# Ordering GpSimd's tensor operations behind VectorE's in a planned attention and mixture-of-experts kernel

## The chip, the cores and the metric

One core of a Trainium2 chip runs the whole program. The metric is device time in microseconds; three runs of the kernel before took 801.38, 801.94 and 803.85 us, so the median is 801.94 us. The profile is of one further execution, 803.63 us long.

## The reference: what is computed

Attention over 4 batches of 8 heads, 576 positions and 64 channels, in which heads 0 to 3 look at the last 32 positions and heads 4 to 7 at every 32nd; its output, 2304 rows of 512, goes through four experts, each weighted per row:

```python
scores = np.where(mask, scale * q @ k.T, -1e9)
attn = softmax(scores); x = (attn @ v)            # -> 2304 x 512
p = domain_probs / (domain_probs.sum(-1, keepdims=True) + 1e-09)
for e in range(4):                                # w1[e] 512 x 1024, w2[e] 1024 x 512
    out += p[:, e:e + 1] * (np.maximum(x @ w1[e], 0.0) @ w2[e])
```

## The kernel before

Everything is float32. A product of two float32 operands is made of three matmuls on rounded halves: each operand is split into a high half (ScalarE rounds it, `AF.Copy`) and a low half (the operand minus its high half), and high x high, high x low and low x high are added in PSUM. The low half is a subtraction of two SBUF operands, and either VectorE or GpSimd may do it; the same holds for most sums and differences of operands.

The rows are treated in three parts. The first 384 rows go through the experts by plain products while attention runs (to about 199 us). The other 1920 are two parts of 896 and 1024 rows (199 to about 492 us, and to the end). Those use a scheme of seven products for a 2 x 2 block product, on halves of the rows (448 or 512 columns of a matmul): per unit (half an expert, 8 units a part) seven products for the hidden layer and seven for the output, each for two halves of the output columns, six matmuls each. [...]

In part 1 the sums of the weights are made too (lines 855, 859 and 862), spilled to DRAM by SP (lines 912 and 921) and read back in part 2 (1149, 1364). GpSimd's queue also issues the DMAs that add a group's output to DRAM (1332, 1335).

The order of all this is not written by hand: the class `Plan` is a list scheduler in Python that runs when the program is built. Each operation has an engine (or a choice: kind `VP` may go to VectorE or GpSimd, kind `AD` to ScalarE or VectorE), an estimated duration, a priority and its dependences. `walk` steps through simulated time: for each engine it looks for the operations that could start first, lets `elsewhere` refuse those which the other engine would finish earlier, picks one by priority, and books it. At the end all operations are issued in order of planned time, each into its engine's queue. The engines then run their queues in order, with semaphores for true dependences only, so that the real overlap of two engines is not bound to the planned one.

Operations with two SBUF inputs carry `two`. Where GpSimd and VectorE both run such an operation, the plan lengthens them (`took`, `slowed`). `harm` estimates how much time VectorE would have in such operations during a GpSimd one; from 45 us on (`EARLY`) `elsewhere` refuses GpSimd an operation by it:

```python
if e == "POOL" and s >= self.EARLY and harm(o, s) > self.SHARE * o.dur[0]:
    return True
```

with `SHARE` 0.0. VectorE's pick goes by priority, except that operations on PSUM go first while GpSimd is known to be busy for more than `NEAR` with an operation on two SBUF inputs.

Of the kernel before, what the change touches and what calls it, by code (L numbers as in the profile page):

```python
# [17 lines left out]
MIX = 2.42  # L18
# [19 lines left out]


class Op:  # L40
    __slots__ = ("eng", "dur", "fn", "nxt", "wait", "ready", "prio", "bank", "start", "end", "moe", "cols", "idx", "xfer", "two", "pre", "kind", "lead", "early", "lag")


class Plan:
# [6 lines left out]
    BUSY, WARM = 3200, 2000  # L51
    LANES, RING = 8, 2048
    DEEP = 1.26
    SHARE = 0.0
    EARLY = 45.0
    NEAR = 0.3
    DEEPER = 5.0
    ROW = 1.0
    SWITCH = 0.17
# [2 lines left out]
    ENGINES = ("PE", "ACT", "DVE", "POOL", "SP")  # L62
    FLEX = {"VP": ("DVE", "POOL"), "AD": ("ACT", "DVE")}

    def __init__(self, banks, mix):
        self.ops = []
        self.number = 0
        self.writer = {}
        self.readers = {}
        self.banks = banks  # L70
        self.mix = mix
        self.swing = self.SWING
# [43 lines left out]
    def run(self, idle):  # L116
# [7 lines left out]
        for n, fn in self.walk():  # L124
            if n:
                idle(n, fn)
            else:
                fn()

    def walk(self):  # L130
        avail = {e: [] for e in self.ENGINES}
        moe = [o for o in self.ops if o.moe]
# [9 lines left out]
        began = False  # L142
        out = []
        seen = {}

        def warm(t):
            k = int(t / self.TICK)
            return k > 0 and seen.get(k - 1, 0) >= self.WARM
# [40 lines left out]
        def when(o):  # L189
            t = o.ready  # L190
            if o.xfer is not None and o.start is None:
                t = max(t, wire - (self.DEEP if wire < 200 else self.DEEPER))
            for i, key in enumerate(o.bank):
                n = len(allocs[key[0]]) - self.banks[key[0]] + i
                if n >= 0:
                    for p in self.readers.get(allocs[key[0]][n], ()):
                        if p.start is None:
                            return None
                        t = max(t, p.end + self.SYNC)
            return t  # L200
# [9 lines left out]
        def took(o, e, s):  # L210

            d = o.dur
            if o.eng in self.FLEX:
                d = d[self.FLEX[o.eng].index(e)]
            if o.two and e in ("DVE", "POOL"):
                other = "POOL" if e == "DVE" else "DVE"
                x = free[other] - s
                if x > 0 and last[other] is not None and last[other].two:
                    d = slowed(s, x, d) if e == "DVE" else d + min(x, d) * 0.2
            return d  # L220

        def harm(o, s):

            t, end = max(free["DVE"], s), s + o.dur[1]
            both = 0.0
            if last["DVE"] is not None and last["DVE"].two:
                both = max(0.0, t - max(s, last["DVE"].start))
            for y in sorted((y for y in avail["DVE"] if y is not o and y.ready < end and y.eng != "AD"), key=lambda y: (y.prio, y.idx)):
                if t >= end:
                    break  # L230
                t = max(t, y.ready)
                d = y.dur[0] if y.eng == "VP" else y.dur
                if y.two:
                    both += max(0.0, min(end, t + d) - t)
                t += d
            return 0.65 * both

        def elsewhere(o, e, s):

            if o.eng not in self.FLEX:  # L240
                return False
            a, b = self.FLEX[o.eng]
            x = b if e == a else a
            if e == "POOL" and s >= self.EARLY and harm(o, s) > self.SHARE * o.dur[0]:
                return True
            est = free[x]
            for y in avail[x]:
                if y is not o and (y.prio, y.idx) < (o.prio, o.idx) and y.eng not in self.FLEX and y.ready < s + 1.0:
                    est += y.dur
            est = max(est, o.ready)  # L250
            return est + took(o, x, est) < s + took(o, e, s) - 1e-9

        def transfer(s, dur, parts):
# [23 lines left out]
        while left:  # L277
            best = None
            for e in self.ENGINES:
                f = free[e]  # L280
                cand = [(max(t, f), o) for t, o in ((when(o), o) for o in avail[e]) if t is not None]
                cand = [c for c in cand if not elsewhere(c[1], e, c[0])]
                if e == "PE" and moe and not moe[-1].wait:
                    t = when(moe[-1])
                    if t is not None:
                        cand.append((max(t, f), moe[-1]))
                if not cand:
                    continue
                s0 = min(c[0] for c in cand) + 1e-9
                if e == "DVE" and s0 > self.EARLY and last["POOL"] is not None and last["POOL"].two and free["POOL"] > s0 + self.NEAR:  # L290
                    pick = min((c for c in cand if c[0] <= s0), key=lambda c: (c[1].two, c[1].prio, c[1].idx))
                elif e == "PE":
                    pick = min((c for c in cand if c[0] <= s0),
                               key=lambda c: (s0 > STEADY and c[1].moe != turn, c[1].prio, c[1].idx))
                else:
                    pick = min((c for c in cand if c[0] <= s0), key=lambda c: (c[1].prio, c[1].idx))
                if best is None or pick[0] < best[0]:
                    best = pick + (e,)
            s, o, e = best
            if e == "PE":  # L300
                f = free["PE"]
                if o.moe:
                    credit = min(credit + o.dur, 8.0)
                    began = True
                else:
                    credit = max(credit - o.dur * self.mix, -8.0)
                row = 0.0 if o.moe else row + o.dur
                if abs(credit) > self.swing:
                    turn = credit < 0
                if row > self.ROW:  # L310
                    turn = True
                if s < STEADY:
                    f = max(f, 1.07)
                    tag = next((t for t in allocs if not (o.bank and o.bank[0][0] == t) and clear(t, f) and not (began and t == "mo")), None)
                    n, f2 = fill(f, s, o) if tag else (0, f)
                    if n:
                        out.append((f, -1, n, tag))
                        allocs[tag].append(("idle",))
                        s = max(s, f2)
            fn = o.fn  # L320
            dur = took(o, e, s)
            if e == "PE" and o.moe and last[e] is not None and not last[e].moe:
                dur += self.SWITCH
            if o.eng in self.FLEX:
                for x in self.FLEX[o.eng]:
                    avail[x].remove(o)
                o.eng = e
                fn = lambda fn=fn, e=e: fn(e)
            elif o.moe:
                moe.pop()  # L330
            else:
                avail[e].remove(o)
            o.start = s
            o.end = stream(s, dur, o.cols) if e == "PE" else s + dur
            free[e] = o.end
            last[e] = o
            if e == "POOL" and o.two and last["DVE"] is not None and last["DVE"].two and free["DVE"] > s:
                d = last["DVE"]
                x = d.end - max(s, d.start)
                d.end += min(d.end - s, dur / 2) if s < self.EARLY else min(x / 0.35, x + 0.65 * dur) - x  # L340
                free["DVE"] = d.end
                for x in d.nxt:
                    if x.start is None:
                        x.ready = max(x.ready, d.end + self.SYNC)
            if o.xfer is not None:
                o.end, free[e] = transfer(s, dur, o.xfer)
            for x in o.nxt:
                x.wait -= 1
                x.ready = max(x.ready, o.end + x.lag + (self.SYNC + self.DRAIN * (e == "PE") if x.eng != e or o.xfer is not None else 0.0))
                if not x.wait:  # L350
                    offer(x)
            for key in o.bank:
                allocs[key[0]].append(key)
            out.append((s, o.idx, 0, fn))
            left -= 1
# [5 lines left out]
def attn_moe_kernel(  # L361
# [38 lines left out]
    BANKS = {"mo": 4, "sc": 2, "ps": 2}  # L400
# [61 lines left out]
    WHOLE = (1,)  # L462
    order = [(b, c) for b in range(B) for c in KORD]
    NP = len(order)
    plan = Plan(BANKS, MIX)
    add = plan.add

    def engine(e):
# [380 lines left out]
    VP = (0.69, 1.28)  # L849
# [596 lines left out]
    key = ("ps", "pr")  # L1446
# [49 lines left out]
    with tc.manual_schedule():  # L1496
# [5 lines left out]
        for t in pm["L"]:  # L1502
            nc.gpsimd.memset(t, 0.0)
            a = t[:, 0:1]
# [83 lines left out]
```

## Time and profile before

| what | value |
|---|---|
| median of three runs | 801.94 us |
| profiled execution | 803.63 us, span 801.9 us |
| TensorE busy | 775.0 us (97%) |
| VectorE busy | 652.5 us (81%) |
| ScalarE busy | 380.7 us (47%) |
| GpSimd busy | 353.5 us (44%) |
| mean granted TensorE clock | 0.990 |
| DMA | 212.67 MB, 265 GB/s on the mean |

In the profile PE is TensorE's matmuls, PEld its weight loads, DVE is VectorE, ACT is ScalarE, POOL is GpSimd and SP is SyncE. A line of a group reads: source line, engine, operation, what it writes <- what it reads, shapes, count, then busy time, mean duration of one in ns, idle time of the engine before it, and what ended that. Durations of VectorE's operations in a timeline overlap by some hundredths of a microsecond, since one begins while the one before drains.

### The profile page before, as it was taken

How to read it: one execution, taken by the hardware profiler on the slowest of the kernel's cores; microseconds unless marked ns; L12 is line 12 of the kernel's file. 1: busy time of each engine (PE TensorE's matmuls, PEld its weight loads, DVE VectorE, ACT ScalarE, POOL GpSimd, SP SyncE). 2: the span in 40 equal slices, each digit the busy share in tenths (PEclk: the TensorE clock that was granted, in tenths of full speed). 3: DMA queues.
4: the chain of work that ended last, by engine and by line, in shares of the span. 5: the costliest groups of instructions: out<-in, count | busy, mean ns of one | idle time of the engine just before them, and what ended most of it. 6: DMA issues, size and time to landing. Idle time of an engine off the chain costs nothing.

```text
span 801.9 us, 14121 instructions
## 1 busy us (share of the span) xinstructions
PE 775.0 (97%) x5374; PEld 666.4 (83%) x5377; DVE 652.5 (81%) x935; ACT 380.7 (47%) x718; POOL 353.5 (44%) x287
## 2 busy tenths in 40 slices
PE   7999999989999999989998989999999999999998
PEld 4788888879998999879987878888888888888786
DVE  6867777897888998998997998848774976499985
ACT  4645544653746375345724663635173435432330
POOL 5414212382666874765666587201010241034562
PEclk9999999999999999998999999999999999999999
DMA  9999999769998797899968746948492788469524
GB/s 335 319 392 401 336 330 337 245 195 374 333 364 299 280 374 267 257 250 338 338 158 255 239 151 119 370 168 319 161 360 84 283 162 336 159 223 247 212 79 157
DMA packets 89630, 212.67 MB, mean 265 GB/s; under 512 B 7071, under 2 KB 33883, under 8 KB 89563
## 3 DMA queue, kind: packets, MB, share of 16 engines
q1 hardware_dynamic: 83659, 201.96, 69.5%
q0 software_dynamic: 5760, 9.70, 8.1%
q8 instruction: 42, 0.69, 0.3%
q14 instruction: 25, 0.20, 0.1%
q10 hardware_dynamic: 144, 0.11, 0.1%
HBM read 138.58 MB, written 73.17 MB: 264 GB/s over the span
## 4 chain that ended last, share of the span: by engine, by line
PE 78%; DVE 11%; issue 3%; DMA 3%; POOL 2%; ACT 2%; SPq 1%; DVEq 0%; POOLq 0%; ACTq 0%
PE mo L1124 21%; PE ps L1124 21%; PE sc L1124 18%; PE mo L954 8%; PE mo L938 7%; DVE T L1211 2%; DVE q L1253 2%; PE ps L741 2%; DVE acc L1321 1%; DMA raw<-in_w 1%; DMA vstL<-in_v_first 1%; DVE ring L855 1%; DVE q L1172 1%; POOL po L1332 1%; PE sc L586 1%
## 5 line engine op out<-in xcount | busy, mean ns | idle before, releaser
L1124 PE MATMUL sc<-T,ring 128*128 128x448 f32 (+2 forms) x774 | 178.9, 380 | 7.3 <-DVE acc L1321 3.3
L1124 PEld LDWEIGHTS sc<-T,ring 128*128 128x128 f32 x774 | 146.6, 191 | 30.6 <-issue 3.8
L1209 ACT ACTIVATE T<-q 128x512 fp32r<-128x512 f32 (+1 forms) x196 | 111.3, 600 | 81.3 <-DVE q L1253 35.2
L1211 DVE TENSOR_TENSOR T<-q,T 128x512 fp32r<-128x512 f32 (+1 forms) x141 | 129.5, 939 | 17.7 <-ACT T L1209 17.2
L1253 POOL TENSOR_TENSOR q<-q,q 128x512 f32<-128x512 f32 (+1 forms) x44 | 65.5, 1497 | 155.6 <-ACT q L1176 137.3
L1211 POOL TENSOR_TENSOR T<-q,T 128x448 fp32r<-128x448 f32 (+1 forms) x55 | 75.6, 1385 | 62.8 <-ACT T L1209 61.5
L1176 ACT ACTIVATE q<-q 128x448 f32<-128x448 f32 (+1 forms) x84 | 50.3, 599 | 94.1 <-DVE q L1172 93.4
L1124 PE MATMUL mo<-T,ring 128*128 128x512 f32 (+1 forms) x396 | 91.3, 379 | 0.7 <-DVE acc L498 0.7
L1172 DVE TENSOR_TENSOR q<-ps,v 128x448 f32<-128x448 f32 (+1 forms) x96 | 62.6, 653 | 35.4 <-PE ps L1124 29.8
L1124 PEld LDWEIGHTS mo<-T,ring 128*128 128x128 f32 x396 | 74.7, 189 | 12.3 <-DVE acc L498 1.4
L954 PE MATMUL mo<-w2t,hs 128*128 128x512 f32 x288 | 72.7, 400 | 2.1 <-DVE hs L945 1.8
L1163 ACT ACTIVATE v<-mo 128x448 f32<-128x448 f32 (+1 forms) x96 | 54.2, 564 | 26.3 <-PE mo L1124 26.0
L954 PEld LDWEIGHTS mo<-w2t,hs 128*128 128x128 f32 x288 | 52.2, 188 | 14.8 <-DVE hs L945 3.0
L1321 DVE TENSOR_TENSOR acc<-sc,acc 128x512 f32<-128x512 f32 (+1 forms) x85 | 54.4, 650 | 10.3 <-PE sc L1124 10.1
L1253 DVE TENSOR_TENSOR q<-q,q 128x512 f32<-128x512 f32 (+1 forms) x56 | 56.4, 1010 | 0.7
L938 PE MATMUL mo<-xh,a 128*128 128x384 f32 x192 | 45.4, 340 | 0.1
L1124 PE MATMUL ps<-t4h,a 128*128 128x448 f32 (+1 forms) x128 | 37.5, 393 | 6.2 <-DVE q L1172 6.2
L1321 DVE TENSOR_TENSOR acc<-mo,acc 128x512 f32<-128x512 f32 (+1 forms) x52 | 33.6, 651 | 10.9 <-PE mo L1124 9.2
L1124 PE MATMUL ps<-T,ring 128*128 128x448 f32 (+1 forms) x180 | 40.9, 376 | 0.1
L496 ACT ACTIVATE acc<-sc 128x448 f32<-128x448 f32 (+1 forms) x36 | 20.4, 568 | 39.9 <-PE sc L1124 39.4
L1124 PEld LDWEIGHTS ps<-T,ring 128*128 128x128 f32 x180 | 33.6, 188 | 5.3 <-DMA ring<-d24a 0.5
L1124 PE MATMUL ps<-t2h,s 128*128 128x448 f32 (+1 forms) x128 | 35.2, 376 | 0.0
(179 smaller groups left out, 1522.1 us busy)
## 6 DMA issues: line engine op xcount, KB each, us to landing
raw<-in_w SPq DMA_DIRECT2D x28, 1024.0 KB, 8.3
qkS<-in_qk_strided SPq DMA_DIRECT2D x16, 329.0 KB, 7.6
vstL<-in_v_local SPq DMA_DIRECT2D x6, 640.0 KB, 9.7
po<-acc POOLq DMA_DIRECT2D x16, 224.0 KB, 6.4
vstS<-in_v_strided SPq DMA_DIRECT2D x8, 384.0 KB, 8.3
a<-d16a SPq DMA_DIRECT2D x6, 512.0 KB, 7.2
ring<-d27a SPq DMA_DIRECT2D x6, 512.0 KB, 6.5
a<-d10a SPq DMA_DIRECT2D x6, 512.0 KB, 4.8
```

The lines of the kernel that those rows point to most:

```text
L496: nc.scalar.activation(out=dst(), in_=src(held[key]), func=AF.Copy)
L741: nc.tensor.matmul(oo[hf][64 * h:64 * h + 64, o:o + w], a, pt[r, x, c0:c0 + w], start=True, stop=True)
L938: nc.tensor.matmul(pt[:, 0:TA], w[:, c % 2, (f % 2) * P:(f % 2) * P + P], (xl if i == 1 else xh)[c], start=j == 0, stop=j == 11)
L954: nc.tensor.matmul(pt, ht[f][:, ts], wt[f][:, cs], start=j == 0, stop=j == 11)
L1124: nc.tensor.matmul(pt, a[i == 2][:, j, f * P:f * P + P], skewed(b[i == 1][j], TH)[:, cs], start=bool(first) and n == 0, stop=True, skip_gr ...
L1163: add("ACT", TH / 1200 + 0.18, lambda: nc.scalar.activation(out=late["u"][i][:, 0:TH], in_=held[key][:, 0:TH], func=AF.Copy), [key, "late2 ...
L1172: add("DVE", DD, lambda: nc.vector.tensor_tensor(out=q(), in0=src(), in1=late["u"][i][:, 0:TH], op=ALU.add), [key, f"u{i}", "late2"], [tok ...
L1176: add("ACT", TH / 1200 + 0.2, lambda: nc.scalar.activation(out=q(), in_=q(), func=AF.Relu), ["late2"], [tok], zs)
L1209: add("ACT", TH / 1200 + 0.17, lambda src=src, hi=hi: nc.scalar.activation(out=hi(), in_=src(), func=AF.Copy), [tok, "late2"], [f"T{i}h{j} ...
L1211: add("VP", vp, lambda e, src=src, hi=hi, lo=lo: engine(e).tensor_tensor(out=lo(), in0=src(), in1=hi().bitcast(F32), op=ALU.subtract), [to ...
L1253: add("VP", vp, lambda e, d=d, x=x, y=y: engine(e).tensor_tensor(out=d[0](), in0=x[0](), in1=y[0](), op=ALU.subtract), [x[1], y[1]], [d[1] ...
L1321: add("DVE", DD, lambda av=av, key=key: nc.vector.tensor_tensor(out=av(), in0=held[key][:, 0:TH], in1=av(), op=ALU.add), [key], tok, zd)
```

## The change

Four things change, all from 45 us on. A GpSimd operation of kind `VP` remembers the latest VectorE operation on two SBUF inputs that was booked before it (`anchor`); in the plan it starts after that one's end, and in the program it waits for it by a semaphore. `SHARE` goes from 0.0 to 0.5, so that a GpSimd operation may be placed where its planned overlap costs VectorE up to half of the operation's own VectorE duration. When VectorE asks whether GpSimd would be earlier, the anchor and the same `harm` test now count. And VectorE's pick is grouped: if more than one operation on PSUM is ready, or one has been ready for over 0.7 us (`HOLD`), those go first; otherwise the operations on two SBUF inputs go first.

```diff
-    SHARE = 0.0
+    SHARE = 0.5
+    HOLD = 0.7
...
+    def issue(self, fn, o):
+
+        ran = fn()
+        o.ins = None if ran is None else ran.ins
+        if o.after is not None and o.ins is not None and o.after.ins is not None:
+            self.tc.add_manual_dep(
+                o.ins, o.after.ins.name, mybir.DependencyInfo(mybir.DependencyClass.Sync, mybir.DependencyReason.DATA),
+                reason="GpSimd behind a VectorE operation on SBUF")
...
-            for y in sorted((y for y in avail["DVE"] if y is not o and y.ready < end and y.eng != "AD"), key=lambda y: (y.prio, y.idx)):
+            for y in sorted((y for y in avail["DVE"] if y is not o and y.ready < end and y.eng != "AD"), key=lambda y: (y.two, y.prio, y.idx)):
...
             est = max(est, o.ready)
+            if x == "POOL" and s >= self.EARLY:
+                if anchor is not None:
+                    est = max(est, anchor.end + self.SYNC)
+                if harm(o, est) > self.SHARE * o.dur[0]:
+                    return False
...
+                if e == "POOL" and anchor is not None and f >= self.EARLY:
+                    cand = [(max(t, anchor.end + self.SYNC) if o.eng == "VP" else t, o) for t, o in cand]
...
+                elif e == "DVE" and s0 > self.EARLY:
+                    now = [c for c in cand if c[0] <= s0]
+                    single = [c for c in now if not c[1].two]
+                    first = len(single) > 1 or any(s0 - c[1].ready > self.HOLD for c in single)
+                    pick = min(now, key=lambda c: (c[1].two == first, c[1].prio, c[1].idx))
...
+            if e == "DVE" and o.two:
+                anchor = o
+            o.after = anchor if e == "POOL" and o.kind == "VP" and s >= self.EARLY else None
...
+            if o.two:
+                fn = lambda fn=fn, o=o: self.issue(fn, o)
```

## Rows read from the trace of the kernel before

**Rows 1.** The page's fourth part: shares of the chain that ended last, by engine.
```profile
PE 78%; DVE 11%; issue 3%; DMA 3%; POOL 2%; ACT 2%; SPq 1%; DVEq 0%; POOLq 0%; ACTq 0%
```

**Rows 2.** Windows: length, busy PE, PEld, DVE, ACT, POOL (instructions), clock, DMA share, GB/s.
```profile
45.00:160.00 115.00, 115.00 (x1860) 97.34 (x1860) 86.08 (x148) 56.21 (x111) 33.00 (x25) 1.00 0.94 340
160.00:199.00 39.00, 36.85 (x181) 32.12 (x180) 34.52 (x42) 18.21 (x37) 20.80 (x15) 1.00 0.81 279
199.00:492.00 293.00, 279.66 (x1348) 255.93 (x1347) 265.93 (x350) 155.20 (x300) 197.12 (x148) 0.98 0.81 270
492.00:740.00 248.00, 248.00 (x1095) 205.32 (x1095) 182.94 (x258) 111.35 (x195) 49.52 (x44) 1.00 0.73 237
```

**Rows 3.** The chain in order of time: start, us, what; undisturbed pieces of both parts.
```profile
208.87 2.40 PE ps L1124 x12
...
505.39 2.72 PE mo L1124 x12
```

**Rows 4.** Waits from 199 to 492 us: who waited for whom, total us, times, longest.
```profile
POOL T L1211 <- ACT T L1209: 30.5, 14, 7.3
...
PE ps L1124 <- DVE q L1172: 6.2, 3, 3.2
...
PE sc L1124 <- DVE acc L1321: 3.3, 3, 1.6
...
PEld ps L1124 <- DMA ring<-d24a: 0.5, 1, 0.5
```

**Rows 5.** The chain around the largest stall, and two VectorE operations on PSUM.
```profile
354.12 5.71 DVE ring L855
...
360.42 2.61 PE ps L1124 x6
...
401.91 1.06 DVE q L1241 x2
```

**Rows 6.** Timeline of VectorE before that stall: start, us, operation, count.
```profile
351.60 0.69 DVE L859 TENSOR_TENSOR tmp<-raw,tmp 128x512 f32<-128x512 f32 x1
...
352.74 0.62 DVE L1211 TENSOR_TENSOR T<-q,T 128x448 fp32r<-128x448 f32 x1
```

**Rows 7.** Timeline of GpSimd during it.
```profile
353.29 1.62 POOL L859 TENSOR_TENSOR tmp<-tmp,raw 128x512 f32<-128x512 f32 x1
354.55 1.46 POOL L1211 TENSOR_TENSOR T<-q,T 128x448 fp32r<-128x448 f32 x1
...
357.87 1.40 POOL L1253 TENSOR_TENSOR q<-q,q 128x448 f32<-128x448 f32 x1
```

**Rows 8.** Windows behind two stalls (columns as in rows 2).
```profile
360.00:366.00 6.00, 5.58 (x15) 4.96 (x16) 6.00 (x10) 3.79 (x8) 2.73 (x2) 0.50 0.80 278
...
428.00:434.00 6.00, 3.18 (x16) 2.65 (x15) 4.94 (x6) 1.54 (x4) 4.23 (x4) 1.00 0.91 241
434.00:438.00 4.00, 4.00 (x15) 3.56 (x14) 4.00 (x5) 2.77 (x7) 4.00 (x3) 0.60 0.72 291
```

**Rows 9.** Timelines of VectorE and of GpSimd around 429 us.
```profile
429.06 1.76 DVE L859 TENSOR_TENSOR tmp<-raw,tmp 128x512 f32<-128x512 f32 x1 [4.25 <-POOL ring L855]
...
426.83 0.87 POOL L1332 DMA_DIRECT2D po<-acc  x1 [4.63 <-issue]
```

**Rows 10.** The chain at 162 us: a GpSimd operation that waited for VectorE.
```profile
161.99 0.85 DVE t1l L1067
...
162.98 0.10 POOL tmp L859
```

**Rows 11.** Groups from 199 to 492 us: VectorE's first and last, GpSimd's first.
```profile
L1211 DVE TENSOR_TENSOR T<-q,T 128x448 fp32r<-128x448 f32 x55 | 57.0, 1047 | 2.3 <-ACT T L1209 1.9
...
L1111 DVE TENSOR_TENSOR b21l<-raw,b21h 128x512 fp32r<-128x512 f32 x1 | 0.7, 675 | 0.0
...
L1211 POOL TENSOR_TENSOR T<-q,T 128x448 fp32r<-128x448 f32 x41 | 55.5, 1364 | 31.8 <-ACT T L1209 30.5 <-DMA raw<-in_w 1.1
```

**Rows 12.** Waits of SP's queue from 199 to 492 us.
```profile
SPq L921 <- POOL ring L855: 24.8, 7, 7.5
```

More of the change, by code (lines that the diff above doesn't have):

```diff
@@ L40 @@
 class Op:
-    __slots__ = ("eng", "dur", "fn", "nxt", "wait", "ready", "prio", "bank", "start", "end", "moe", "cols", "idx", "xfer", "two", "pre", "kind", "lead", "early", "lag")
+    __slots__ = ("eng", "dur", "fn", "nxt", "wait", "ready", "prio", "bank", "start", "end", "moe", "cols", "idx", "xfer", "two", "pre", "kind", "lead", "early", "lag", "after", "ins")
 class Plan:
@@ L63, with __init__ @@
     FLEX = {"VP": ("DVE", "POOL"), "AD": ("ACT", "DVE")}
-    def __init__(self, banks, mix):
+    def __init__(self, banks, mix, tc):
+        self.tc = tc
         self.ops = []
@@ L144, in walk @@
         seen = {}
+        anchor = None
         def warm(t):
@@ L464, in attn_moe_kernel @@
     NP = len(order)
-    plan = Plan(BANKS, MIX)
+    plan = Plan(BANKS, MIX, tc)
     add = plan.add
```

## The prediction

> **What bounds the kernel now.** I read the page's chain first: TensorE is 78% of the chain that ended last, VectorE 11% [rows 1]. So TensorE sets the time, and only the stretches in which it waits can be won. The windows by stage [rows 2] say where: from 45 to 160 us TensorE is busy for all 115.00 us, from 492 to 740 for all 248.00; from 160 to 199 it idles 39.00 - 36.85 = 2.15 us, and from 199 to 492 (called part 1 here) 293.00 - 279.66 = 13.3 us; there its granted clock is 0.98 on the mean, so 0.02 x 293 = 5.9 us more went at half clock. Where nothing disturbs part 1, the chain is a row of 12 matmuls in 2.40 us [rows 3]; part 1 has 8 units x 14 products x 2 row halves x 6 matmuls = 1344, or 112 such pieces: 268.8 us. It takes 293, so 24.2 us are lost in it; idle time and half clock are 19.2 of them, the rest lies in stretched pieces around the stalls. The list of waits puts 6.2 and 3.3 us of TensorE's idle time down to VectorE alone [rows 4].
>
> The largest stall shows the mechanism. At 354.12 one VectorE subtraction on two SBUF inputs takes 5.71 us, and one eviction after it TensorE goes on [rows 5]. VectorE had done the same kind of work in 0.62 us just before [rows 6]. During the 5.71 us GpSimd ran to the end of one operation and started four more, 1.11 us apart [rows 7]; the VectorE operation ended 0.56 us after the last of them. It was passed over four times, and the evictions behind it with it. [...] A second stall looks alike but is not: at 429 VectorE had waited 4.25 us for a GpSimd subtraction that stood behind an accumulating DMA issue on GpSimd's queue, and that issue came after 4.63 us in which GpSimd waited for nothing that the profile shows [rows 9]. With the lower clock behind it, it cost 2.82 + 0.4 x 4 = 4.4 us [rows 8].
>
> **The change, part by part.**
> *The waits.* Part 1 has 148 GpSimd instructions [rows 2]; 20 are DMA issues by the groups of its lines, so 128 tensor operations gain a wait on a VectorE operation. The hand-over has a row: a GpSimd operation began 0.14 us after the end of the VectorE one that it waited for [rows 10]. The wait proper lies between nothing (VectorE is done already) and one VectorE operation, 0.62 us; I take half, 0.31. That is 128 x 0.45 = 58 us against the 293 - 197 = 96 us for which GpSimd now idles in part 1 [rows 2], and its operations should shorten from 1364 ns [rows 11] towards the 1.11 us of rows 7: 128 x 0.25 = 32 us back. So GpSimd's idle time hides the waits on the mean. Behind a waiting operation stand GpSimd's later operations, ScalarE's roundings of their results, and the 20 DMA issues; what those write is wanted a group of two units (some 70 us) later, so they cost nothing unless GpSimd falls behind for good. SP's queue waits too: it now spends 24.8 us on waits for GpSimd's `ring` halves before their spills [rows 12], with reloads queued behind; the plan orders a reload 14 us ahead of its use, and that is the cover. Without it the price would be that of the late reload there is now, 0.5 us [rows 4].
>
> *The collisions that go.* Of VectorE's 350 operations in part 1, 179 have two SBUF inputs: twelve groups, of which rows 11 shows the largest and the last. Against the solo 0.62 us (0.68 for 512 columns) [rows 6] the largest loses 55 x (1.047 - 0.62) = 23.5 us; all twelve, worked out alike, 68. Without them VectorE's 265.9 us [rows 2] are 198. GpSimd's 128 operations need 128 x 1.11 = 142 us beside VectorE operations that read PSUM; there are 171 of these, one per 0.53 us back to back [rows 5], or 91 us. For the missing 51 us VectorE idles or still collides. So VectorE needs about 249 us, and up to 267 if the hand-overs (128 x 0.14 = 18) land on it too, of TensorE's 268.8: under the bound, but at 93 to 99% of it. Demand comes in bursts, so some stalls stay. Of the 24.2 us I set aside 4.4 (GpSimd's DMA issue) and 0.5 (the reload); about 19 belong to VectorE's backlog. I take two thirds of them as gone, 13 us, since a VectorE this full leaves no room for all. Ends: 0 and 19.
>
> [...]
>
> *Share 0.5, and the same test from both engines.* Before, GpSimd took an operation only where the plan saw no overlap, and VectorE could leave it to GpSimd all the same; now a little overlap is allowed and VectorE keeps what GpSimd would refuse. Operations move between the engines, each for 0.62 us of VectorE's time. Bounds: some 10 of the 128 either way, 6 us, covered by TensorE unless VectorE is late. I take nothing.
>
> *Grouping of PSUM operations.* A lone one may now wait 0.7 us and one operation on SBUF, 1.3 us in all; two or more go first. Cover: a bank is used again two products later, 2.40 us [rows 3] and half a product, so 1.3 us fits. Where nothing covers it, at the end of the first stage (the correction of the hidden layer, L945, with 2.15 us of idle time around it [rows 2]), it can take up to 3 us or give back the 2. I take nothing, ends -2 and +3. In part 2 (492 to 740) VectorE is busy for 183 of 248 us and TensorE never waits [rows 2]: nothing can be won, and a loss needs a delay of more than a piece, 2.72 us [rows 3].
>
> **Sum.** -13 us. The profiled execution took 803.63 us (the span of 801.9 and 1.7 around it), so 790.6; the median of the three runs, 801.94, lies 1.7 below the profiled one, hence 789.
>
> **The rivals.**
> 1. *GpSimd becomes late (slower).* If the mean wait passes 96 / 128 = 0.75 us, GpSimd's idle time in part 1 is used up: an operation whose VectorE partner is itself held by ScalarE or TensorE holds everything behind it. Then the low halves of a next product come late, as at 429, which cost 4.4 us. With a third of the gain kept (-4) and three such stalls more (+13.2): 811. For: GpSimd already waits most for ScalarE's roundings, 30.5 us in 14 waits [rows 4], so its work arrives in bursts and has little slack at their ends. Against: 96 us of idle time, and shorter operations. 24%.
> 2. *The waits change nothing.* Either the partner is always done before GpSimd's own inputs are, or the two engines swap who is late: 802. For: GpSimd's operations are stretched as well, 1364 ns against 1.11 us [rows 7, 11], so both already pay, and the work on SBUF stays the same. Against: what is lost is the evictions queued behind a held VectorE operation, and those a wait on GpSimd sets free. 13%.
> 3. *All backlog goes.* 19 us, and the 2 us before 199: 781, counted from the profiled time as above. It needs VectorE at its lower figure and even demand. 8%.
>
> **How the numbers follow.** The forecast has 55%, with a range of its own of 780 to 799. A measurement of this kernel can tell 0.3%, 2.4 us, from no change. Faster by more: 55 + 8 = 63%. Within: 13%. Slower: 24%. The whole range runs from 777 (rival 3 with twice its 2 us before 199) to 809; this leaves out a few hundredths below and the upper part of rival 1, some 14%.
>
> **What would show it.** Right: in part 1 VectorE's `T` subtractions (L1211) fall from 1047 ns to under 800; no VectorE operation on SBUF exceeds 2 us; GpSimd's fall under 1250 ns; TensorE's idle time there falls from 13.3 us to about 5, and its clock is 0.99 or more. Wrong: VectorE is freed but TensorE idles as before with GpSimd as the releaser (rival 1); the VectorE means stay above 1000 ns (rival 2); or stalls of TensorE appear between 45 and 160 or 492 and 740 us, where there are none: then the new order of the plan costs more than its waits.

## The result, and the profile after

The changed kernel takes 780.39 us (median of four runs, 779.86 to 781.02), the kernel before in the same comparison 801.66 us: a ratio of 0.9735, with a 95% interval of 0.9707 to 0.9763. A second comparison gave 779.73 against 803.24 us, 0.9721 (0.9698 to 0.9744). The forecast was 789, with 781 for the rival in which all of VectorE's backlog goes. The profiled execution took 780.38 us, its span is 778.6.

The chain that ended last, by engine (to be read beside rows 1): VectorE's share has gone from 11% to 4%.
```profile
PE 91%; DVE 4%; DMA 2%; issue 1%; POOL 1%; ACT 0%; DVEq 0%; ACTq 0%; POOLq 0%
```
The windows by stage (columns as in rows 2):
```profile
45.00:160.00 115.00, 114.92 (x1861) 97.47 (x1860) 86.55 (x149) 57.26 (x114) 24.86 (x19) 1.00 0.92 337
160.00:199.00 39.00, 39.00 (x197) 35.32 (x196) 35.28 (x56) 20.60 (x40) 3.74 (x3) 1.00 0.85 309
199.00:492.00 293.00, 289.88 (x1433) 267.95 (x1432) 257.86 (x420) 173.06 (x332) 112.25 (x99) 1.00 0.85 288
492.00:740.00 248.00, 248.00 (x1096) 205.42 (x1095) 182.59 (x273) 104.15 (x184) 36.21 (x33) 1.00 0.70 235
```
From 199 to 492 us TensorE idles 3.1 us instead of 13.3 and its clock is 1.00 instead of 0.98 [rows 2]; its only waits there are these, three in all (to be read beside rows 4):
```profile
PE ps L1153 <- DVE q L1201: 3.1, 3, 1.9
```
By the first and last matmul of 448 columns in the timelines, part 1 now runs from 196.83 to 469.93, 273.1 us, where it ran from 199.10 to 491.75, 292.65 us. So 19.55 us come from part 1, 2.27 from before it (the idle 2.15 us of 160 to 199 are gone) and the remaining 1.4 from after it: together the 23.25 us between the two profiled executions. Of the 24.2 us that part 1 lost against 268.8, 4.3 are left.

What the operations did, from 199 to 476 us (lines are numbered 29 higher than before; columns as in rows 11):
```profile
L1240 DVE TENSOR_TENSOR T<-q,T 128x448 fp32r<-128x448 f32 x66 | 43.5, 675 | 2.5 <-ACT T L1238 2.3
...
L1240 POOL TENSOR_TENSOR T<-q,T 128x448 fp32r<-128x448 f32 x30 | 34.8, 1168 | 63.8 <-ACT T L1238 50.5 <-DVE T L1240 3.6 <-DMA a<-d11a 3.6
```
VectorE's mean fell from 1047 to 675 ns, GpSimd's from 1364 to 1168, and a count that the forecast had left nearly still moved most: GpSimd has 73 tensor operations in part 1 instead of 128 (the sum of its groups). VectorE does the rest, and yet over its part 1 it is busy 25 us less: 392 instructions in 240.78 us, where 350 took 265.93 [rows 2].
```profile
197.00:470.00 273.00, 269.88 (x1346) 251.61 (x1345) 240.78 (x392) 159.04 (x308) 103.26 (x90) 1.00 0.84 289
```
The time by which VectorE's operations on two SBUF inputs in part 1 exceed 0.62 us (0.68 for 512 columns), which was 68 us before, is now 17 us.

The stall that the prediction set aside is still there (to be read beside rows 9): GpSimd's queue issues an accumulating DMA late, this time after a wait for a spill to land (`d24s<-ring`), VectorE waits 4.40 us for a subtraction behind it, and TensorE idles 1.9 us, the longest of the waits above.
```profile
417.98 0.69 DVE L888 TENSOR_TENSOR tmp<-raw,tmp 128x512 f32<-128x512 f32 x1 [4.40 <-POOL ring L884]
...
415.76 0.87 POOL L1361 DMA_DIRECT2D po<-acc  x1 [1.67 <-DMA d24s<-ring]
416.32 1.62 POOL L884 TENSOR_TENSOR ring<-tmp,ring 128x512 fp32r<-128x512 f32 x1
```

### The profile page after: what moved, and what is told of

The parts are those of the page before. It is cut to its first block, busy times and chain, and to the rows that moved or that the text cites. A ratio compares the mean times of both kernels' runs of the same rounds, so it can differ in the third digit from the quotient of the medians.

```text
span 778.6 us, 14138 instructions
## 1 busy us (share of the span) xinstructions
PE 764.6 (98%) x5374; PEld 663.4 (85%) x5377; DVE 623.0 (80%) x1015; ACT 384.6 (49%) x725; POOL 209.4 (27%) x200
## 4 chain that ended last, share of the span: by engine, by line
PE 91%; DVE 4%; DMA 2%; issue 1%; POOL 1%; ACT 0%; DVEq 0%; ACTq 0%; POOLq 0%
PE mo L1153 25%; PE ps L1153 24%; PE sc L1153 20%; PE mo L983 9%; PE mo L967 8%; PE ps L770 2%; DMA d24s<-ring 1%; PE sc L626 1%; PE ps L738 1%; PE sc L615 1%; DMA raw<-dx 1%; DVE T L1240 1%; PE mo L1523 1%; DVE ring L884 0%; DVE q L1282 0%
## 5 line engine op out<-in xcount | busy, mean ns | idle before, releaser
L1153 PE MATMUL sc<-T,ring 128*128 128x448 f32 (+2 forms) x774 | 174.4, 374 | 0.0
L1153 PEld LDWEIGHTS sc<-T,ring 128*128 128x128 f32 x774 | 144.5, 188 | 19.8 <-DVE T L1240 0.2
L1240 DVE TENSOR_TENSOR T<-q,T 128x512 fp32r<-128x512 f32 (+1 forms) x154 | 105.8, 703 | 15.6 <-ACT T L1238 15.1
L1240 POOL TENSOR_TENSOR T<-q,T 128x448 fp32r<-128x448 f32 (+1 forms) x42 | 50.3, 1205 | 93.1 <-ACT T L1238 73.1
L1282 POOL TENSOR_TENSOR q<-q,q 128x512 f32<-128x512 f32 (+1 forms) x13 | 16.6, 1273 | 183.2 <-DVE T L1240 166.5
L1282 DVE TENSOR_TENSOR q<-q,q 128x448 f32<-128x448 f32 (+1 forms) x87 | 58.1, 679 | 1.9 <-ACT q L1205 1.2
L525 ACT ACTIVATE acc<-sc 128x448 f32<-128x448 f32 (+1 forms) x41 | 23.2, 567 | 46.4 <-PE sc L1153 45.1
L1153 PE MATMUL ps<-t4h,a 128*128 128x448 f32 (+1 forms) x128 | 35.3, 377 | 2.3 <-DVE q L1201 2.3
L1153 PE MATMUL ps<-t3h,s 128*128 128x448 f32 (+1 forms) x128 | 35.2, 377 | 0.9 <-DVE q L1201 0.9
```

What stands on the lines that cost most here:

```text
L525: nc.scalar.activation(out=dst(), in_=src(held[key]), func=AF.Copy)
L1153: nc.tensor.matmul(pt, a[i == 2][:, j, f * P:f * P + P], skewed(b[i == 1][j], TH)[:, cs], start=bool(first) and n == 0, stop=True, skip_gr ...
L1240: add("VP", vp, lambda e, src=src, hi=hi, lo=lo: engine(e).tensor_tensor(out=lo(), in0=src(), in1=hi().bitcast(F32), op=ALU.subtract), [to ...
L1282: add("VP", vp, lambda e, d=d, x=x, y=y: engine(e).tensor_tensor(out=d[0](), in0=x[0](), in1=y[0](), op=ALU.subtract), [x[1], y[1]], [d[1] ...
```

## The experiments

The change has four parts, of which only one reaches the chip as such: the semaphore waits. The others (the anchor in the plan, SHARE with VectorE's own test, the grouping) only make another plan. "Held" below is the time by which VectorE's operations on two SBUF inputs exceed 0.62 us (0.68 for 512 columns), added up over part 1 as long as it lasts in that run. Profile rows are windows from 199 to 492 us, waits of TensorE in that window, and groups of L1211's operation, whatever its line. After each time stands its ratio to the kernel before in the same comparison, with a 95% interval.

**1. The changed plan without its waits.** Engines and queue orders are those of the changed kernel.
```diff
-        if o.after is not None and o.ins is not None and o.after.ins is not None:
+        if False:
```


> The changed kernel with the order of every queue and the engine of every operation kept, and only the added semaphore waits left out. Theory A (the waits keep GpSimd from passing a held VectorE operation, as predicted): most of the gain goes, 793 to 802 us, VectorE operations of several us come back. Theory B (the plan gives GpSimd half as many operations, so that VectorE is rarely held at all): 780 to 785 us, VectorE's mean on two SBUF inputs in part 1 stays under 800 ns.

779.09 us, ratio 0.9707 (0.9688 to 0.9727).
```profile
199.00:492.00 293.00, 290.75 (x1436) 268.80 (x1436) 264.18 (x423) 172.97 (x333) 122.06 (x99) 1.00 0.86 290
...
L1240 DVE TENSOR_TENSOR T<-q,T 128x448 fp32r<-128x448 f32 (+1 forms) x73 | 49.4, 692 | 2.2 <-ACT T L1238 1.9
L1240 POOL TENSOR_TENSOR T<-q,T 128x448 fp32r<-128x448 f32 (+1 forms) x31 | 39.0, 1271 | 61.5 <-ACT T L1238 56.9 <-PE ps L1153 4.0 <-DVE T L1258 0.6
```
Nothing of the gain goes. The waits do what they say: without them GpSimd's `T` operations are 1271 ns instead of 1172 in the same window, VectorE is held 21 us instead of 17 and is busy 264.2 us instead of 257.9. But TensorE idles no more for it. Theory A falls.

**2. The waits alone, on the old plan.** Every queue keeps its old order. Since GpSimd may here be planned to start before a VectorE operation booked earlier, the wait is for the latest one that the plan starts before it.
```diff
+            o.after = max((a for a in anchors if a.start < s), key=lambda a: a.start, default=None) if e == "POOL" and o.kind == "VP" and s >= self.EARLY else None
```


> The kernel before with every queue in its old order and every operation on its old engine, each GpSimd operation from 45 us on also waiting for the latest VectorE operation on two SBUF inputs that the plan starts before it. Theory A: 783 to 792 us, the 5.71 us operation gone. Theory B: 798 to 812 us, since 128 operations on GpSimd in part 1 fill its queue and now wait too; a gain of at most a few us.

802.16 us, ratio 1.0005 (0.9989 to 1.0021).
```profile
199.00:492.00 293.00, 280.43 (x1359) 256.61 (x1358) 254.89 (x347) 155.89 (x300) 183.60 (x144) 0.98 0.79 271
...
L1228 DVE TENSOR_TENSOR T<-q,T 128x448 fp32r<-128x448 f32 x55 | 54.6, 1001 | 3.1 <-ACT T L1226 2.5
L1228 POOL TENSOR_TENSOR T<-q,T 128x448 fp32r<-128x448 f32 x41 | 52.8, 1298 | 33.0 <-DVE tmp L876 13.7 <-DVE T L1228 9.4 <-ACT q L1193 4.6
```
GpSimd does wait for VectorE (13.7 and 9.4 us before this group alone), VectorE's mean falls only from 1047 to 1001 ns, held 57 us, and TensorE idles 12.6 us as against 13.3. The timelines of VectorE and GpSimd show why:
```profile
356.10 0.68 DVE L872 TENSOR_TENSOR ring<-tmp,ring 128x512 fp32r<-128x512 f32 x1
...
357.30 3.75 DVE L876 TENSOR_TENSOR tmp<-raw 128x512 f32<-128x512 f32 x1
```
```profile
356.65 1.62 POOL L876 TENSOR_TENSOR tmp<-tmp,raw 128x512 f32<-128x512 f32 x1
357.90 1.48 POOL L1228 TENSOR_TENSOR T<-q,T 128x448 fp32r<-128x448 f32 x1
359.02 1.48 POOL L1270 TENSOR_TENSOR q<-q,q 128x448 f32<-128x448 f32 x1
```
GpSimd's first operation starts when VectorE's `ring` is nearly through, and it still runs when VectorE's next one starts, at 357.30; two more GpSimd operations, whose partners lie earlier, pass that one too. A wait looks back at the operation before; the one that pays, here with 3.75 us for 0.68, is the next.

**3. The change without the grouping.** VectorE picks by priority as before.
```diff
-                elif e == "DVE" and s0 > self.EARLY:
-                    now = [c for c in cand if c[0] <= s0]
...
-            for y in sorted((... key=lambda y: (y.two, y.prio, y.idx)):
+            for y in sorted((... key=lambda y: (y.prio, y.idx)):
```


> The change without VectorE's new pick (and without the key of its estimate): VectorE picks by priority as before. Theory C (grouping opens the windows in which GpSimd runs free): over 792 us and collisions back above 1000 ns. Theories A and B: 778 to 787 us, since the waits and the placement stay.

790.81 us, 0.9849 (0.983 to 0.9868), which no theory had expected. Part of the gain goes, but not into collisions: VectorE is held 21 us, and its `T` mean is 685 ns. TensorE's idle time in part 1 has another releaser:
```profile
PE mo L1148 <- ACT s L878: 8.4, 2, 4.9
```
That is ScalarE's rounding of a weight sum. On the chain behind each of these two stalls stands a load of weights (`raw<-in_w`). The one behind the shorter takes 12.25 us from 202.18 on; the one behind the longer SP issued at 410.65, after a spill whose inputs VectorE had just made:
```profile
410.41 0.17 SPq L936
...
410.68 12.16 DMA raw<-in_w
```
So this plan loses most of its 10 us to two late loads and to the lower clock behind them (0.80 from 217 to 224 us, 0.72 from 424 to 430). The experiment shows that the grouping matters in this plan, and not that it opens windows for GpSimd.

**4. VectorE alone.** No operation of the free kind goes to GpSimd after 45 us.
```diff
-            if e == "POOL" and s >= self.EARLY and harm(o, s) > self.SHARE * o.dur[0]:
+            if e == "POOL" and s >= self.EARLY:
...
-                if harm(o, est) > self.SHARE * o.dur[0]:
+                if True:
```


> The change with no operation of the free kind on GpSimd after 45 us: VectorE does them all. No collisions at all. By the count of rows before, part 1 asks of VectorE 307 operations at 0.6 us and 171 at 0.53 us, about 275 us against TensorE's 268.8. If the placement on VectorE is the whole of the gain (theory B at its limit): 778 to 786 us. If GpSimd's share is still needed (theory A): 788 to 805 us, VectorE busy without a break in part 1 and TensorE waiting for it.

794.40 us, 0.9895 (0.987 to 0.992), in the range for a GpSimd whose share is still needed.
The page's busy times of the whole run, and the `T` group:
```profile
PE 770.0 (97%) x5377; PEld 663.5 (84%) x5377; DVE 657.4 (83%) x1137; ACT 383.5 (48%) x726; POOL 56.0 (7%) x77
...
L1240 DVE TENSOR_TENSOR T<-q,T 128x448 fp32r<-128x448 f32 x96 | 57.6, 616 | 3.8 <-ACT T L1238 3.7
...
PE mo L1153 <- ACT s L883: 3.9, 2, 2.7
PE sc L1153 <- DVE T L1240: 2.7, 5, 1.2
```
Without a collision after 45 us VectorE does all 1137 instructions in 657.4 us; before, 935 took it 652.5, with GpSimd doing most of the rest. GpSimd's share had saved VectorE 5 us. The time is 8 us better without them and 14 us worse than with those that the change leaves to GpSimd, so placed help is worth something: TensorE here waits again, for low halves from VectorE and for weight sums, as the last two rows show.

**5. The grouping alone**, on the kernel before: VectorE's new pick, nothing else.


> The kernel before with VectorE's new pick alone: no waits, no anchor in the plan, SHARE 0.0; GpSimd keeps 218 of 228 tensor operations in the whole program. Theory D (the anchor in the plan takes half of GpSimd's operations away, and that is the gain; grouping only helps beside it): 797 to 804 us. Theory C (grouping by itself opens windows): 786 to 794 us, as much as the 10 us that leaving it out cost.

812.09 us, 1.0107 (1.0071 to 1.0143): 1% slower, beyond both theories. VectorE is held 61 us, nearly as before. TensorE idles 19.2 us instead of 13.3; its wait for `q` is the 6.2 us of rows 4, and the waits for the output's accumulation have grown (3.3 us there):
```profile
199.00:492.00 293.00, 273.85 (x1318) 250.46 (x1318) 252.03 (x341) 156.33 (x301) 181.14 (x136) 0.98 0.79 271
...
PE ps L1146 <- DVE q L1194: 6.2, 3, 3.4
PE sc L1146 <- DVE acc L1343: 5.6, 3, 2.9
```

**6. The change without the anchor**, in plan and program; grouping, SHARE 0.5 and VectorE's own test stay.
```diff
-                if anchor is not None:
-                    est = max(est, anchor.end + self.SYNC)
...
-                if e == "POOL" and anchor is not None and f >= self.EARLY:
-                    cand = [(max(t, anchor.end + self.SYNC) if o.eng == "VP" else t, o) for t, o in cand]
```


> The change without the anchor, in the plan as in the program: grouping, SHARE 0.5 and VectorE's own test of the overlap stay; GpSimd has 231 tensor operations again instead of 141. Theory D: 794 to 804 us, collisions as before. Theory C: 779 to 788 us.

810.34 us, 1.0095 (1.0077 to 1.0113): slower than both theories expected. GpSimd has 123 tensor operations in part 1, VectorE is held 60 us, and TensorE idles 20.8 us, mostly for evictions:
```profile
199.00:492.00 293.00, 272.24 (x1312) 249.91 (x1310) 255.29 (x349) 158.28 (x306) 178.68 (x136) 0.97 0.79 268
...
PE sc L1149 <- ACT acc L521: 5.9, 1, 5.9
PE sc L1149 <- DVE acc L523: 4.0, 1, 4.0
PE sc L1149 <- DVE acc L1346: 3.8, 2, 3.6
```

**7. The anchor in the plan alone**: the lines removed in 6 added to the kernel before, no waits, no grouping, SHARE 0.0.


> The kernel before with the anchor in the plan alone (GpSimd's operation is planned behind VectorE's, and VectorE's estimate of GpSimd's time counts that): no waits, no grouping, SHARE 0.0, no test of the overlap from VectorE's side; GpSimd keeps 107 tensor operations. Theory D: 786 to 794 us, near the 790.8 that the change without grouping takes. Theory C: 798 to 803 us.

786.19 us, 0.979 (0.9776 to 0.9805), in theory D's range.
```profile
199.00:492.00 293.00, 289.56 (x1422) 264.85 (x1421) 265.39 (x438) 170.90 (x324) 90.60 (x76) 1.00 0.85 285
...
L1233 DVE TENSOR_TENSOR T<-q,T 128x448 fp32r<-128x448 f32 x80 | 54.6, 701 | 4.1 <-ACT T L1231 3.9
```
Some three quarters of the gain (16.5 of 21 to 24 us) come from one rule of the plan. GpSimd keeps 53 operations in part 1, VectorE is held 16 us, TensorE idles 3.4 us there.

**8. The change without waits and with SHARE 0.0.**
```diff
-    SHARE = 0.5
+    SHARE = 0.0
```


> The change without its waits and with SHARE 0.0 again: no planned overlap is allowed, GpSimd has 100 tensor operations, 41 fewer, which VectorE does. Theory D with an optimum: between the 779.1 us of 141 and the 794.4 us of none on GpSimd, about 782 to 788 us. If fewer is simply better: under 779 us.

790.16 us, 0.9834 (0.9811 to 0.9856), outside both ranges. GpSimd keeps 50 operations in part 1, VectorE is held 17 us. The 11 us over experiment 1 lie in stalls of TensorE behind one eviction (3.8 us), one `T` subtraction (2.6) and a late reload (2.3 us), and in the clock behind them:
```profile
199.00:492.00 293.00, 282.97 (x1382) 260.38 (x1381) 258.14 (x428) 162.59 (x315) 87.02 (x72) 0.99 0.82 275
...
PE ps L1153 <- DVE q L1201: 4.3, 3, 3.8
PE sc L1153 <- DVE T L1240: 2.6, 1, 2.6
PE ps L1153 <- DMA ring<-d22a: 2.3, 1, 2.3
```
With 7 beside it (SHARE 0.0 too, and 4 us faster without the grouping and VectorE's own test), differences of this size between neighbouring plans are not put down to one rule here.

**9. The number alone.** The kernel before, with three of five free operations kept on VectorE by their number in the plan, so that GpSimd has as many as in the change.
```diff
-            if e == "POOL" and s >= self.EARLY and harm(o, s) > self.SHARE * o.dur[0]:
+            if e == "POOL" and s >= self.EARLY and (o.idx % 5 in (0, 2, 4) or harm(o, s) > self.SHARE * o.dur[0]):
...
+            if x == "POOL" and s >= self.EARLY and o.idx % 5 in (0, 2, 4):
+                return False
```


> The kernel before with three of every five operations of the free kind (by their number in the plan) kept on VectorE after 45 us, so that GpSimd has 138 tensor operations, as many as in the change, with no anchor, no grouping, no waits and SHARE 0.0. If the number alone is the gain (theory D1): 784 to 792 us, as with the anchor but without grouping (790.8 and 786.2). If it is the place behind VectorE's operation (theory D2): 796 to 806 us, with more collisions per GpSimd operation than the change has.

801.33 us, 0.9967 (0.995 to 0.9985), in theory D2's range.
```profile
199.00:492.00 293.00, 280.34 (x1348) 257.10 (x1347) 270.02 (x396) 157.22 (x303) 124.72 (x96) 0.97 0.80 269
...
L1213 DVE TENSOR_TENSOR T<-q,T 128x448 fp32r<-128x448 f32 x73 | 58.6, 819 | 0.4 <-ACT T L1211 0.2
...
PE mo L1126 <- DVE T L1213: 4.2, 1, 4.2
```
GpSimd has 77 operations in part 1, nearly the 73 of the change, but VectorE is held 47 us, 0.61 us for each of them; in experiment 1, which has no waits either, it is 0.29. They still come in runs, as VectorE's and GpSimd's timelines before the stall of 4.2 us show:
```profile
467.27 3.05 DVE L1213 TENSOR_TENSOR T<-q,T 128x448 fp32r<-128x448 f32 x2
470.24 1.68 DVE L1255 TENSOR_TENSOR q<-q,q 128x448 f32<-128x448 f32 x1
```
```profile
466.83 1.53 POOL L1255 TENSOR_TENSOR q<-q,q 128x448 f32<-128x448 f32 x1
468.32 1.52 POOL L1213 TENSOR_TENSOR T<-q,T 128x448 fp32r<-128x448 f32 x1
469.80 1.64 POOL L1113 TENSOR_TENSOR b21l<-raw,b21h 128x512 fp32r<-128x512 f32 x1
```
So the number is not the gain; which operations the anchor leaves on GpSimd, and when, is. The traces show the when: the first VectorE operation that begins during one of GpSimd's in part 1 reads PSUM for 68 of 128 before and 36 of 77 here, but for 60 of 73 in the changed kernel, 53 of 73 in experiment 1 and 36 of 53 in experiment 7.

**10 to 12. The change again, without its waits again, and without VectorE's own test.** The edit of the last, beside the missing waits:
```diff
-                if harm(o, est) > self.SHARE * o.dur[0]:
-                    return False
```


> The changed kernel itself once more, beside the next one on the same chip: 779 to 782 us.

779.73 us, 0.9721 (0.9698 to 0.9744).

> The changed kernel without its added waits once more. If the waits cost nothing and give nothing: within 1 us of the one before it. If leaving them out is worth the 1.3 us of the first comparison: 778 to 780 us, below it beyond the interval.

781.17 us, 0.9723 (0.9696 to 0.975). In the first comparison the kernel without waits was 1.3 us ahead, now it is 1.4 behind, which neither range had: the waits make no difference that these runs can tell.

> The change without its waits and without VectorE's own test of the overlap; the anchor, grouping and SHARE 0.5 stay, GpSimd has 140 tensor operations. If that test only tidies the plan: 777 to 783 us. If it is needed, because an operation that both engines refuse is put off in the plan: over 785 us.

782.66 us, 0.974 (0.9718 to 0.9763): the test from VectorE's side is worth a microsecond or two at most. No version tried is clearly faster than the changed kernel.

Over all of them one split holds: with the anchor in the plan VectorE is held 16 to 25 us and the kernel takes 779 to 791 us (the change and experiments 1, 3, 7, 8 and 10 to 12); with GpSimd in use and no anchor it is held 47 to 68 us and the kernel takes 801 to 812 us (before and experiments 2, 5, 6 and 9).

## Why the prediction was right, and where it was not

The time came out inside the range by luck as to the cause. The waits, from which the 13 us were worked out, are worth nothing that the runs can tell; by them alone the kernel takes 802 us. Another part of the change, to which the prediction gave no time, brought the gain.

*What bounds the kernel: right.* The 24.2 us lost in part 1 were the place, and 19.55 of the 23.25 us came from there. Before, most of TensorE's idle time there ended on VectorE [rows 4]; the largest stall, 3.2 us of idle time [rows 4], had a granted clock of 0.50 behind it from 360 to 366 us [rows 8]. Between 45 and 160 and 492 and 740 us TensorE is as busy as it was (114.92 and 248.00 us).

*The waits: the step that failed.* The prediction let the 128 waits take the collisions away. They take away few (experiment 2: VectorE held 57 us instead of 68, and 802.16 us, the 802 of rival 2) and the gain does not need them (experiments 1 and 11). The rows held the reason: in rows 5 and 7 GpSimd was running when the VectorE operation began. By the starts in the trace of before, GpSimd was already running in 90 of the 106 collisions of part 1 (overlaps of more than 0.06 us), and these held VectorE for 66 of the 68 us; in 16 VectorE had started first, and they cost it 1.6. A wait for a VectorE operation that came before can only prevent the 16, and turn GpSimd's runs into shorter ones. In the new plan it does the first: VectorE is first in 17 collisions without the waits (experiment 1) and in one with them, and GpSimd in 46 and 38. Nor did the held operation of rows 5 go on when the GpSimd operation in flight had ended: that one ended at 354.91, VectorE's at 359.83, 0.56 us after the last of four more [rows 7].

*The plan's rules: mis-sized.* "I take nothing" for operations that move, with 10 of 128 as the bound: 55 moved. The anchor reads as the plan's side of a wait, but in a list scheduler it delays every GpSimd candidate to the end of VectorE's current operation, and then VectorE, asked in turn, is often earlier. Alone it gives 786.19 us (experiment 7). Moving as many by number gives 801.33 (experiment 9), so it is not the relief of GpSimd but the choice: what stays on GpSimd mostly starts as VectorE turns to PSUM (the counts under experiment 9), and each GpSimd operation holds VectorE about half as long (0.29 us in experiment 1 against 0.61 in experiment 9). In part 1 of the kernel before VectorE's operations of 448 columns that read PSUM took 613 ns on the mean with a GpSimd operation beside them (123, overlaps of more than 0.06 us) and 615 without (46). The remaining 5 us or so come only with SHARE 0.5 and the grouping together (786 us with neither, 790 and 791 with one of them). Why this is so stays open, since these plans differ by late loads and single stalls as well (experiments 3 and 8).

*The size.* 13 us were forecast from part 1 on the ground that a VectorE at 93 to 99% leaves no room for all of its 19. It was not that full: 240.8 of the 273 us of part 1, 88%, since the plan's anchor avoids most collisions, and that saves VectorE more than the 55 operations cost that it takes over. The two thirds were too low, and rival 3's 781 us was the time. The 4.4 us set aside for GpSimd's late DMA issue became one stall of 1.9 us of idle time.

*The rivals.* Rival 1 (GpSimd late) did not occur: with 73 operations GpSimd idles 181 of 293 us. Plans slower than before exist (experiments 5 and 6, 812 and 810 us, with GpSimd nearly as full as before), but GpSimd itself ends only 1.1 and 0.7 us of TensorE's waits there. *Grouping*, taken as nothing with ends of -2 and +3, is worth +9 us alone, some -10 beside the anchor with SHARE 0.5 (experiment 3) and, together with VectorE's own test, +4 beside it with SHARE 0.0 (8 against 7), by late loads and evictions and not by collisions.

*The signs named.* VectorE's mean under 800 ns, GpSimd's under 1250, TensorE's idle time near 5 and its clock above 0.99: all came, though their cause was another. The longest VectorE operation of part 1 is 2.17 us, not under 2. Without the waits they come just the same, but for GpSimd's mean (1271 ns in experiment 1). Such signs could hardly tell the waits from the plan; taking the waits out did.

## What to carry to other kernels

Where operations of two engines lengthen as they overlap, count in the trace which of them was first in each collision before adding an order: here VectorE came second in 90 of 106, and a wait of GpSimd for VectorE's earlier operations left 57 of the 68 us (experiment 2). And where a change edits a planner, ask of each edited line how many operations it moves; the count of instructions per engine and window in the new profile is the first row to read, before any mean duration.

## What the runs showed of the hardware

GpSimd beside VectorE was worth almost nothing here before it was placed: 935 VectorE instructions with GpSimd's operations beside them took VectorE 652.5 us, and 1137, with none beside them after 45 us, took 657.4 (experiment 4): 4.9 us for 202 more. In the collisions of part 1 before, it was mostly the engine that came second that took longer. VectorE lost 66 us over the 90 in which GpSimd was first, 0.74 us each, and 1.6 us over the 16 in which it was first itself. A GpSimd operation of 448 columns that followed on no other (over 0.2 us after GpSimd's last) took 1.44 us on the mean when it began inside a VectorE one on two SBUF inputs (15 of them) and 1.15 us clear of them (5). VectorE was passed over by several GpSimd operations in a row, by four for 5.71 us before and by two for 3.75 us in experiment 2. In the traces of before and of the change VectorE and ScalarE alone read PSUM (VectorE's evictions in the two parts are `q` of lines 1172 and 1241, `T` of 1229 and `acc` of 1321 in the kernel before); none of GpSimd's 287 and 200 instructions did.
